# Attention, MoE and GLU on one core: token order scattered inside the GLU, GpSimd's weight splits whole and in other iterations

## The chip, the cores and the metric

The kernel runs on one core of a Trainium2 chip. The metric is the device time of one execution in microseconds (us). The engines are called as in the profile: PE is TensorE (matmuls; PEld its weight loads), DVE is VectorE, ACT is ScalarE, POOL is GpSimd and SP is SyncE, which here only issues DMAs. Each engine works through its own instructions in program order; semaphores tie them together.

## What is computed

Three stages follow each other, all in float32: sliding-window attention with four sink tokens, a top-1 mixture of eight experts with a capacity, and a gated linear unit (GLU).

```python
scores = where(is_sink | in_window, q @ k.T / sqrt(64), -1e9)    # 2 x 8 heads, 768 tokens
x = softmax(scores) @ v                                          # -> [1536, 512]

e = argmax(x @ w_gate, axis=1)                                   # top-1 of 8 experts
disp[e, counts[e]] = x[i]       # the first 384 tokens of each expert, in order of token
y = relu(disp @ w1) @ w2        # 512 -> 1024 -> 512
x[i] = gate_w[i] * y[e, pos[i]] # 0 for tokens over the capacity

out = (sigmoid(x @ w_gate2) * (x @ w_val)) @ w_out               # 512 -> 1536 -> 512
```

## The kernel before

Matmuls are float32 products made of three products each (`mm3`, lines 174 to 177): an operand is split into a high part and the rest. The split of a weight tile is `split_w` (lines 132 to 140): ACT copies the raw tile (`staged`, 128x1024) into the high half of a `pair` tile (L135), and another engine subtracts that from the raw tile into the low half (L140). Raw tiles come by DMA on SP's queue (`load_w`) into four stage buffers of two tiles each.

**Attention** (lines 180 to 684) goes through 12 tiles of 128 tokens, six for each of two sequences. A loop over `n` = 0 to 23 takes half the heads of tile `i = n // 2` in an iteration. In one iteration PE makes the `scores` of `n` (L288), the transposes of iteration n-1 (L321) and the products with `v` of n-2 (`pv`, L342, with a sink product L380); DVE adds the masks (L296) and ACT takes the exponentials (L307). An odd iteration ends with the sinks (`sink_gather`: two copies on ACT, L363, and a subtraction `psk` on DVE, L366, both of whose inputs lie in SBUF) and with `place` of tile i-2, whose first DVE instruction gives `pos_all` (L460) and frees the bank of PSUM that the next scores need. Iteration 15, the odd one of the second sequence's second tile, also splits that sequence's sink rows on DVE (`vsh`, L259 and L260).

POOL copies `v` at even iterations (`place_v`, L218), computes slot numbers, scales and scatters the rows of tile i-2 to the experts' slots in DRAM at odd ones (L467 to L481), and in ten iterations makes the split of one weight tile. These ten are picked by the list `splits` (line 578): from 6 on, without tile 6 (12 and 13) and without 15, so 6 to 11, 14, 16, 17 and 18. Two iterations after each, SP loads the tile that takes the place of the split one. When POOL makes a split, it is cut into four subtractions of 128x256.

**The token order.** A token's row in the experts' output differs from its row in the result. For each tile of tokens, `pi` (a sum of two tables, made by DVE) says where in the order its tokens went; POOL scatters the token numbers there, 128 at a time, by an indirect DMA into a table `idsd` in DRAM (`order_ids`, lines 705 to 712). In experts 1 to 6 one call makes two columns of `pi` and two scatters. After the last expert SP loads the whole table as `ids` (`load_ids`, L715), a DMA of 1,536 runs of 4 bytes.

**The experts** (lines 718 to 961) work through 128 to 384 rows each, with branches on the counts, while weights stream in.

**The GLU** (lines 980 to 1181) has three chunks of 512 rows and 12 steps in a chunk. A step `t` multiplies the chunk by a block of two weight matrices (`up`: 24 matmuls, then `g` on ACT and DVE, `gh` on ACT, `gl` on DVE), and then multiplies the step before by the output weights into four accumulators `acc0` to `acc3` (`down`: 12 matmuls). The accumulators are complete after the `down` of a chunk's last step, which runs in the first step of the next chunk; for the first chunk that is step 12, the thirteenth. There `finish` copies each accumulator into a buffer `o` (ACT for 0 and 2, DVE for 1 and 3; three buffers in all) and POOL scatters its rows to the result at the places in `ids` (L1065). The `down` of the next step, the 13th by number, starts the accumulators anew, `acc3` last.

Of the kernel before, what the change touches and what calls it, by code (L numbers as in the profile page):

```python
# [9 lines left out]
F32 = mybir.dt.float32  # L10
# [5 lines left out]
ALU = mybir.AluOpType  # L16
# [5 lines left out]
SUB = 1024  # L22
# [4 lines left out]
def kernel(  # L27
# [16 lines left out]
    nc = tc.nc  # L44
# [6 lines left out]
    NT = S // P  # L51
    NTILE = B * NT
# [8 lines left out]
    AHEAD = 10  # L61
# [31 lines left out]
    pi_a = const.tile([P, NTILE], F32, name="pi_a")  # L93
    pi_d = const.tile([P, NTILE], F32, name="pi_d")
    pi = const.tile([P, NTILE], I32, name="pi")
# [36 lines left out]
    def split_w(i, eng):  # L132

        raw, t = staged(i), pair[i // 2 % NDBL][:, :, i % 2 * SUB:(i % 2 + 1) * SUB]
        nc.scalar.copy(out=t[:, 0], in_=raw)  # L135

        n = 4 if eng is nc.gpsimd else 1
        for j in range(n):
            c = slice(j * SUB // n, (j + 1) * SUB // n)
            eng.tensor_sub(out=t[:, 1, c], in0=raw[:, c], in1=t[:, 0, c].bitcast(F32))  # L140

    def split_next(i, eng):

# [36 lines left out]
    def attention():  # L180
        with ExitStack() as st:
# [85 lines left out]
            NQ = 2 * NTILE  # L267
# [255 lines left out]
            for m, c in ((0, 0), (1, BW), (2, BW)):  # L523
# [3 lines left out]
                    out=blk, in_=blk, pattern=[[-1, P]], compare_op=ALU.is_ge, fill=MASKED,  # L527
# [46 lines left out]

            splits = [n for n in range(6, NQ) if n // 2 != NT and n != 2 * NT + 3][:AHEAD]
            for n in range(NQ):
                i, a = divmod(n, 2)  # L580
                if a == 0:
# [120 lines left out]
        )  # L702
        nc.vector.tensor_tensor(out=pi_a, in0=a, in1=pos_all, op=ALU.add)

    def order_ids(i0, i1):
        c = slice(i0, i1)
        nc.vector.tensor_tensor(out=pi[:, c], in0=pi_a[:, c], in1=pi_d[:, c], op=ALU.add)
        for i in range(i0, i1):
            nc.gpsimd.indirect_dma_start(
                out=idsd_v[i], out_offset=bass.IndirectOffsetOnAxis(ap=pi[:, i:i + 1], axis=0),  # L710
                in_=ids0[:, i:i + 1], in_offset=None, bounds_check=N - 1, oob_is_err=False,
            )

    def load_ids():
        nc.sync.dma_start(out=ids, in_=idsd.rearrange("(j p) o -> p (j o)", p=P))  # L715


    def experts(yh, yl):
        with ExitStack() as st:
# [188 lines left out]
            for e in range(E):  # L908
                w1a, w1b, w2a, w2b = (weights(4 * e + j) for j in range(4))
                m = 8 * e  # L910
                if e:
                    load_x_next(e + 2)
                    load_more(e)
                    split_next(m + 2, V)
                    split_next(m + 3, V)
                u = bank(ps_u, 0)
                go(products(u, x, w1a, True, True))
                ra = relu(u)
                if e:
                    put_y(e - 1, 0, yr)  # L920
                    split_next(m + 4, V)
                else:
                    cnt_x = counts([nc.sync.engine])
                    for j in range(1, E):
                        nc.sync.dma_start(
                            out=slots[j * ROWS:(j + 1) * ROWS, :][bass.ds(cnt_x[j], P), :], in_=zero)
                    load_more(e)
                    load_x_next(2)
                u = bank(ps_u, 0)
                b = products(u, x, w1b, True, True)  # L930
                go(b[:6])
                ha = turn_h(ra, 0)
                if e:
                    split_next(m + 5, V)
                go(b[6:])
                rb = relu(u)
                if e:
                    split_next(m + 6, V)
                if e + 1 < E:
                    x = turn_x(xs[e + 1], 0)  # L940
                y = bank(ps_y, 0)
                a = products(y, ha, w2a, True, False)
                go(a[:6])
                hb = turn_h(rb, 1)
                if e:
                    split_next(m + 7, V)
                go(a[6:])
                if e == 0:
                    cnt_e = counts([nc.tensor.engine, nc.scalar.engine, nc.vector.engine])
                    order(hp)  # L950
                elif e < 7:
                    order_ids(2 * (e - 1), 2 * e)
                fills = [partial(split_w, m + j, V) for j in (8, 9)] if 0 < e < E - 1 else []
                if e + 1 == E:
                    for q in range(4):
                        fills += [partial(whole, q, h * 512, h * 512 + 512) for h in range(2)]
                        if q < 2:
                            fills.append(partial(convert, q))
                yr = more_tiles(e, y, products(y, hb, w2b, False, True), fills)
                if 0 < e < E - 1:  # L960
                    load_w(m + 16)
                    load_w(m + 17)
            load_glu(4, 0)
            load_glu(5, 1)
            load_ids()
            fill_clock(5)
            for q in range(2, 4):
                convert(q)
# [11 lines left out]
    def glu(yh, yl):  # L980
        with ExitStack() as st:
# [36 lines left out]
            def up(n, r, w):  # L1018
                ch = n // NPAIR
                c = slice(r * P, (r + 1) * P)  # L1020
                cols = slice(ch * 512, ch * 512 + w)
                pss = []
                for j in range(2):
                    wh, wl = block(n, j)
                    ps = ps_g.tile([P, 512], F32, tag=f"g{j}", name=f"g{j}")[:, :w]
                    for k in range(KD):
                        mm3(ps, wh[:, k, c], wl[:, k, c], yh[:, k, cols], yl[:, k, cols], k == 0, k == KD - 1)
                    pss.append(ps)
                gh = gp.tile([P, 512], F32R, tag="gh", name="gh", bufs=3)
                gl = gp.tile([P, 512], F32R, tag="gl", name="gl", bufs=3)  # L1030
                g = gp.tile([P, 512], F32, tag="g", name="g")[:, :w]
                nc.scalar.activation(out=g, in_=pss[0], func=AF.Sigmoid)  # L1032
                nc.vector.tensor_tensor(out=g, in0=g, in1=pss[1], op=ALU.mult)  # L1033
                nc.scalar.copy(out=gh[:, :w], in_=g)  # L1034
                k = last_rows(w)
                nc.vector.tensor_sub(out=gl[:, :w - k], in0=g[:, :w - k], in1=gh[:, :w - k].bitcast(F32))  # L1036
                if k:
                    nc.vector.tensor_sub(
                        out=gh[:, w:w + k], in0=g[:, w - k:], in1=gh[:, w - k:w].bitcast(F32)
                    )  # L1040
                return gh, gl
# [48 lines left out]
            def run(t0, t1, w, half, before):  # L1090

                ch = t0 // NF
                held = []

                for m in range((w + P - 1) // P, 4):
                    put_out(ch * 4 + m, zero)
                for t in range(t0, t1):
                    pend = []
                    n, r = steps[t]
                    while half and len(pend) < 3:  # L1100
                        x, h = half[0]
                        if todo[x][0] > n + 2:
                            break
                        half.pop(0)
                        pend.append((x, h))
                    parts = [(x % 4, h * 512, h * 512 + 512) for x, h in pend]
                    for step in range(3):
                        conv_a(parts, step)
                    g = up(n, r, w)
                    for x, h in pend:  # L1110
                        conv_b(x % 4, todo[x][2], h * 512, h * 512 + 512, nc.vector)
                        if h and x + 4 < len(todo):
                            load_glu(todo[x + 4][1], x % 4)
                    if before and t < len(steps) - 2:
                        full = w if t > t0 else 512
                        for m in range((full + P - 1) // P):
                            down(t - 1, m, *before, full)
                        if t % NF == 0:
                            for m in range(4):
                                finish(t // NF - 1, m, full)  # L1120
                    held = (held + [g])[-3:]
                    before = g
                if t1 == len(steps):

                    ms = list(range((w + P - 1) // P))
                    if w % P:
                        ms = ms[-1:] + ms[:-1]
                    for m in ms:
                        down(t1 - 3, m, *held[0], w)
                    for m in ms:  # L1130
                        down(t1 - 2, m, *held[1], w)
                        down(t1 - 1, m, *held[2], w)
                        finish(ch, m, w, m == ms[-1])
                return before
# [117 lines left out]
```

## Time and profile before

| | |
|---|---|
| median of three runs | 642.01 us (640.71 to 644.28) |
| the profiled execution | 642.88 us |
| its span, first to last instruction | 641.0 us |
| mean granted TensorE clock | 0.977 of 2.4 GHz |
| attention / expert 0 / other experts / GLU, from about | 0 / 137 / 194 / 350 us |
| PE, DVE, ACT, POOL busy | 95%, 57%, 47%, 18% of the span |

The profile is of one execution. The page gives each engine's busy time, the clock that TensorE was granted and the DMA engines' load. The trace behind it gives each instruction's start and duration, in us from the span's start, and in brackets how long its engine had been idle before it and what ended that wait.

### The profile page before, as it was taken

To read this page: it belongs to the slowest core of one execution; us is meant where nothing else is said; L and a number is where in the kernel's file an instruction comes from. 1 tells how busy PE (TensorE), PEld (TensorE's weight loads), DVE (VectorE), ACT (ScalarE), POOL (GpSimd) and SP (SyncE) were. 2 spreads that over 40 slices of the span, in tenths; PEclk is the share of its full clock that TensorE was granted. 3 is DMA by queue.
4 is the path that set the end of the run, shared out by engine and by line. 5 is a ranking of instruction groups with operands and counts; after the bars stand their busy time and mean duration, and the time that the engine had idled before them with its cause. 6 is when DMAs were issued, how large, how long until landed. Compare 5 with 4: busy or idle time off the path is not lost.

```text
span 641.0 us, 9386 instructions
## 1 busy us (share of the span) xinstructions
PE 606.8 (95%) x3326; PEld 504.9 (79%) x3326; DVE 365.6 (57%) x884; ACT 303.0 (47%) x586; POOL 114.6 (18%) x191
## 2 busy tenths in 40 slices
PE   9999989999997889898799999999999999999995
PEld 4888888957876667686687788888888888999994
DVE  2565566544269446828567999993218921238811
ACT  3676666613268446737545655542214521225411
POOL 3169778360002010201000000000200000200002
PEclk9998989999999789989989999999999999999999
DMA  8999947033038965957944555453101530103001
GB/s 182 305 292 310 298 143 235 17 126 125 0 108 221 210 237 188 219 170 255 128 178 133 198 195 179 178 179 123 65 1 65 197 132 0 67 0 95 38 0 70
DMA packets 43630, 93.97 MB, mean 147 GB/s; under 512 B 5664, under 2 KB 24352, under 8 KB 39728
## 3 DMA queue, kind: packets, MB, share of 16 engines
q1 hardware_dynamic: 39872, 86.24, 45.8%
q0 software_dynamic: 2304, 6.09, 2.6%
q10 hardware_dynamic: 1392, 0.86, 0.6%
q8 instruction: 34, 0.56, 0.4%
q14 instruction: 28, 0.23, 0.1%
HBM read 82.63 MB, written 10.75 MB: 146 GB/s over the span
## 4 chain that ended last, share of the span: by engine, by line
PE 52%; issue 30%; DVE 6%; DMA 5%; ACT 5%; POOL 1%; SPq 0%; POOLq 0%; ACTq 0%; DVEq 0%
PE u L779 20%; PE pv L342 5%; PE g L176 4%; PE g L177 4%; PE g L175 4%; PE t L321 3%; PE s L288 2%; DMA xe<-slots 2%; PE idle L505 2%; DMA stage<-in_we_dram 2%; PE acc L177 2%; PE acc L176 2%; PE acc L175 2%; DVE pair L140 2%; ACT pt L307 1%
## 5 line engine op out<-in xcount | busy, mean ns | idle before, releaser
L176 PE MATMUL g<-yl,pair 128*128 128x512 f32 (+1 forms) x288 | 108.4, 376 | 0.3 <-DVE yl L812 0.3
L175 PE MATMUL g<-yh,pair 128*128 128x512 f32 (+1 forms) x288 | 108.4, 376 | 0.2 <-ACT yh L811 0.2
L177 PE MATMUL g<-yh,pair 128*128 128x512 f32 (+1 forms) x288 | 108.3, 376 | 0.0
L140 DVE TENSOR_TENSOR pair<-stage,pair 128x1024 fp32r<-128x1024 f32 x54 | 64.8, 1221 | 19.7 <-ACT pair L135 19.4
L779 PE MATMUL u<-pair,hh 128*128 128x512 f32 x224 | 66.1, 423 | 9.2 <-issue 8.0
L1034 ACT CAST gh<-g 128x512 fp32r<-128x512 f32 (+1 forms) x36 | 21.4, 594 | 110.1 <-DVE g L1033 106.1
L1033 DVE TENSOR_TENSOR g<-g,g 128x512 f32<-128x512 f32 (+1 forms) x36 | 23.5, 651 | 82.4 <-PE g L177 82.4
L135 ACT CAST pair<-stage 128x1024 fp32r<-128x1024 f32 x64 | 65.8, 1051 | 0.9 <-PE u L779 0.8
L779 PE MATMUL u<-pair,xh 128*128 128x512 f32 x224 | 62.9, 409 | 0.1
L175 PEld LDWEIGHTS g<-yh,pair 128*128 128x128 f32 x288 | 54.1, 188 | 9.4 <-ACT yh L811 0.7
L176 PEld LDWEIGHTS g<-yl,pair 128*128 128x128 f32 x288 | 54.1, 188 | 8.6 <-issue 0.6
L177 PEld LDWEIGHTS g<-yh,pair 128*128 128x128 f32 x288 | 54.1, 188 | 7.4
L307 ACT ACTIVATE pt<-sc,neg 128x260 f32<-128x260 f32 (+1 forms) x96 | 44.6, 491 | 30.8 <-DVE neg L296 30.2
L779 PEld LDWEIGHTS u<-pair,hh 128*128 128x128 f32 x224 | 43.2, 200 | 20.3 <-issue 10.8
L1065 POOL DMA_INDIRECT out_dram<-o,ids x11 | 10.8, 983 | 246.9 <-DVE gl L1036 151.6
L779 PEld LDWEIGHTS u<-pair,xh 128*128 128x128 f32 x224 | 43.1, 197 | 10.8 <-ACT xh L753 1.3
L177 PE MATMUL acc<-pair,gl 128*128 128x512 f32 x132 | 51.5, 390 | 0.0
L176 PE MATMUL acc<-pair,gh 128*128 128x512 f32 x132 | 51.4, 390 | 0.0
L175 PE MATMUL acc<-pair,gh 128*128 128x512 f32 x132 | 51.4, 389 | 0.0
L1032 ACT ACTIVATE g<-g 128x512 f32<-128x512 f32 (+1 forms) x36 | 20.5, 568 | 60.5 <-PE g L177 60.5
L342 PE MATMUL pv<-v,pts 128*128 128x73 f32 x352 | 43.2, 276 | 0.0
L342 PEld LDWEIGHTS pv<-v,pts 128*128 128x128 f32 x352 | 42.5, 197 | 0.1
(163 smaller groups left out, 1039.1 us busy)
## 6 DMA issues: line engine op xcount, KB each, us to landing
stage<-in_we_dram SPq DMA_DIRECT2D x64, 512.0 KB
stage<-in_wd_dram SPq DMA_DIRECT2D x30, 1024.0 KB
vraw<-in_vr_dram SPq DMA_DIRECT2D x11, 288.0 KB
kraw<-in_kd_dram SPq DMA_DIRECT2D x22, 132.0 KB
qraw<-in_qd_dram SPq DMA_DIRECT2D x22, 128.0 KB
vt<-in_vt_dram SPq DMA_DIRECT2D x11, 256.0 KB
slots<-zero SPq DMA_DIRECT2D x1, 2048.0 KB
xs<-slots SPq DMA_DIRECT2D x8, 256.0 KB
```

Source lines behind the costliest of these rows:

```text
L135: nc.scalar.copy(out=t[:, 0], in_=raw)
L140: eng.tensor_sub(out=t[:, 1, c], in0=raw[:, c], in1=t[:, 0, c].bitcast(F32))
L175: nc.tensor.matmul(ps, ah, bh, start=start, stop=False)
L176: nc.tensor.matmul(ps, ah, bl, start=False, stop=False)
L177: nc.tensor.matmul(ps, al, bh, start=False, stop=stop)
L307: nc.scalar.activation(out=pt_[i][:, h, :w], in_=scs_[n][j][:, :w], func=AF.Exp, scale=-1.0, bias=neg_[i][:, h:h + 1],)
L321: nc.tensor.transpose(tt[:, r, j], pt_[i][:, 4 * a + 2 * p + r, c:c + P], ident)
L342: nc.tensor.matmul(pv_[n][:, h], pts_[n, h // 2][:, h % 2, j], vb[kb][:, 4 * a + h], start=(h == 0 and j == 0), stop=(h == 3 and j == len( ...
L779: nc.tensor.matmul(ps, a, b, start=start, stop=stop)
L1032: nc.scalar.activation(out=g, in_=pss[0], func=AF.Sigmoid)
L1033: nc.vector.tensor_tensor(out=g, in0=g, in1=pss[1], op=ALU.mult)
L1034: nc.scalar.copy(out=gh[:, :w], in_=g)
```

## The change

Three things change. POOL's split is one subtraction of 128x1024. The list of iterations with a split leaves out 12 to 15 in place of 12, 13 and 15, so that it is 6 to 11 and 16 to 19. And `order_ids` makes all twelve columns of `pi` in one DVE instruction and issues all twelve scatters one after the other, in the GLU's step 10 behind `up`; `load_ids` stands in step 12.

```diff
@@ split_w
         nc.scalar.copy(out=t[:, 0], in_=raw)
-
-        n = 4 if eng is nc.gpsimd else 1
-        for j in range(n):
-            c = slice(j * SUB // n, (j + 1) * SUB // n)
-            eng.tensor_sub(out=t[:, 1, c], in0=raw[:, c], in1=t[:, 0, c].bitcast(F32))
+        eng.tensor_sub(out=t[:, 1], in0=raw, in1=t[:, 0].bitcast(F32))
@@ attention
-            splits = [n for n in range(6, NQ) if n // 2 != NT and n != 2 * NT + 3][:AHEAD]
+            splits = [n for n in range(6, NQ) if n // 2 not in (NT, NT + 1)][:AHEAD]
@@
-    def order_ids(i0, i1):
-        c = slice(i0, i1)
-        nc.vector.tensor_tensor(out=pi[:, c], in0=pi_a[:, c], in1=pi_d[:, c], op=ALU.add)
-        for i in range(i0, i1):
+    def order_ids():
+        nc.vector.tensor_tensor(out=pi, in0=pi_a, in1=pi_d, op=ALU.add)
+        for i in range(NTILE):
             nc.gpsimd.indirect_dma_start(
@@ experts
                     order(hp)
-                elif e < 7:
-                    order_ids(2 * (e - 1), 2 * e)
@@
             load_glu(5, 1)
-            load_ids()
             fill_clock(5)
@@ glu, run
                     g = up(n, r, w)
+
+                    if t == 10:
+                        order_ids()
+                    elif t == 12:
+                        load_ids()
                     for x, h in pend:
```

POOL's instructions in attention, from the copy of `v` in iteration 14 to the split of iteration 16, before; `pair` and `stage` are the split's tiles, `xg` the scaled rows, `slots` the experts' rows in DRAM:

```order
L218 COPY v<-vraw 128x8x64
L140 TENSOR_TENSOR pair_90<-stage_86,pair_90 128x256 x4
L455 TENSOR_TENSOR acc<-acc,oh_all 128x8
L467 TENSOR_SCALAR sl<-idf,pos_all 128x1
L471 TENSOR_SCALAR over<-pos_all 128x1
L475 TENSOR_SCALAR si<-over,sl 128x1
L443 TENSOR_SCALAR xg<-x,g 128x512
L481 DMA slots<-xg,si 4096x512
L217 MEMSET v 128x8
L218 COPY v<-vraw 128x8x64
L140 TENSOR_TENSOR pair_90<-stage_86,pair_90 128x256 x4
```

And now, the same stretch (the change's line numbers are 4 to 9 lower):

```order
L214 COPY v<-vraw 128x8x64
L451 TENSOR_TENSOR acc<-acc,oh_all 128x8
L463 TENSOR_SCALAR sl<-idf,pos_all 128x1
L467 TENSOR_SCALAR over<-pos_all 128x1
L471 TENSOR_SCALAR si<-over,sl 128x1
L439 TENSOR_SCALAR xg<-x,g 128x512
L477 DMA slots<-xg,si 4096x512
L213 MEMSET v 128x8
L214 COPY v<-vraw 128x8x64
L136 TENSOR_TENSOR pair_90<-stage_86,pair_90 128x1024
```

The split behind the first copy is gone, the tile that it made is made in iteration 16, and it is one instruction instead of four.

POOL's instructions from the last expert with an order to the first output scatters, before:

```order
L709 DMA idsd<-ids_67,pi 1536x1 x2
L742 UNCONDITIONAL_BRANCH
L879 UNCONDITIONAL_BRANCH
L1065 DMA out_dram<-o,ids 1536x512 x4
L1139 TENSOR_LOAD cnt_i
```

And now:

```order
L736 UNCONDITIONAL_BRANCH
L873 UNCONDITIONAL_BRANCH
L703 DMA idsd<-ids_67,pi 1536x1 x12
L1056 DMA out_dram<-o,ids 1536x512 x4
L1135 TENSOR_LOAD cnt_i
```

All twelve scatters of the order now stand right ahead of the first four output scatters. On DVE the sum that they need stands between `gl` of step 10 and `g` of step 11, two steps ahead of the copies of `acc1` and `acc3`:

```order
L1027 TENSOR_TENSOR gl<-g,gh 128x512
L701 TENSOR_TENSOR pi<-pi_a,pi_d 128x12
L1024 TENSOR_TENSOR g<-g,g_5951 128x512
L1027 TENSOR_TENSOR gl<-g,gh 128x512
L1024 TENSOR_TENSOR g<-g,g_5996 128x512
L1027 TENSOR_TENSOR gl<-g,gh 128x512
L1073 COPY o<-acc_5232 128x512
L1073 COPY o<-acc_5234 128x512
```

Before, there was no `pi` here; the row after `gl` was the next step's `g`.

## Rows read from the trace of the kernel before

**Rows 1.** Order of time, POOL, attention: start, duration (us), line, operation, idle before.
```profile
41.23 0.62 POOL L218 COPY v<-vraw 128x512 f32<-128x512 f32 x1 [4.01 <-DMA vraw<-in_vr_dram]
41.82 2.80 POOL L140 TENSOR_TENSOR pair<-stage,pair 128x256 fp32r<-128x256 f32 x4
...
51.99 2.79 POOL L140 TENSOR_TENSOR pair<-stage,pair 128x256 fp32r<-128x256 f32 x4
...
81.19 3.39 POOL L140 TENSOR_TENSOR pair<-stage,pair 128x256 fp32r<-128x256 f32 x4
```

**Rows 2.** Order of time, DVE, attention.
```profile
41.91 0.68 DVE L366 TENSOR_TENSOR psk<-pt,psk 128x32 fp32r<-128x32 f32 x1 [2.79 <-ACT psk L363]
...
52.42 1.78 DVE L366 TENSOR_TENSOR psk<-pt,psk 128x32 fp32r<-128x32 f32 x1 [2.85 <-ACT psk L363]
...
81.53 1.09 DVE L260 TENSOR_TENSOR vsh<-vsr,vsh 32x512 fp32r<-32x512 f32 x1
...
84.00 0.61 DVE L366 TENSOR_TENSOR psk<-pt,psk 128x32 fp32r<-128x32 f32 x1
```

**Rows 3.** Line L366 as a whole: shortest, median, longest in ns.
```profile
L366 DVE TENSOR_TENSOR psk<-pt,psk x10: 191/207/1785, 22.1 to 125.6; 128x32 fp32r<-128x32 f32 x10
```

**Rows 4.** Order of time, PE, attention: scores.
```profile
47.05 1.17 PE L288 MATMUL s<-kraw,qraw 64*128 64x132 f32 x16
...
54.34 1.00 PE L288 MATMUL s<-kraw,qraw 64*128 64x132 f32 x6 [1.26 <-DVE pos_all L460]
...
59.65 1.17 PE L288 MATMUL s<-kraw,qraw 64*128 64x132 f32 x16
...
81.82 0.72 PE L288 MATMUL s<-kraw,qraw 64*128 64x132 f32 x8
...
84.76 0.71 PE L288 MATMUL s<-kraw,qraw 64*128 64x132 f32 x6 [1.39 <-DVE pos_all L460]
...
90.05 1.17 PE L288 MATMUL s<-kraw,qraw 64*128 64x132 f32 x16
...
95.15 1.26 PE L288 MATMUL s<-kraw,qraw 64*128 64x132 f32 x16
```

**Rows 5.** Stretches: us, busy us (count) of PE, PEld, DVE, ACT, POOL; PEclk; DMA.
```profile
54.62:58.03 3.41, 3.41 (x20) 3.18 (x18) 2.66 (x15) 2.12 (x5) 2.94 (x7) 0.50 1.12 295
85.34:88.75 3.41, 3.41 (x18) 3.34 (x17) 2.35 (x15) 2.71 (x7) 3.00 (x5) 0.50 0.91 226
```

**Rows 6.** Groups by line and shape, POOL: busy us, mean ns, idle before.
```profile
L140 POOL TENSOR_TENSOR pair<-stage,pair 128x256 fp32r<-128x256 f32 x40 | 28.5, 743 | 1.1 <-DVE sum L387 1.0
...
L673 POOL TENSOR_TENSOR tmp<-kd,lower 128x64 f32<-128x64 f32 x1 | 0.3, 335 | 0.0
```

**Rows 7.** Order of time, GLU, around the end of the first chunk.
```profile
439.36 0.69 DVE L1036 TENSOR_TENSOR gl<-g,gh 128x512 fp32r<-128x512 f32 x1 [0.69 <-ACT gh L1034]
...
456.41 0.98 POOL L1065 DMA_INDIRECT out_dram<-o,ids  x1 [151.56 <-DVE gl L1036]
457.69 0.99 POOL L1065 DMA_INDIRECT out_dram<-o,ids  x1 [0.30 <-issue]
...
459.26 0.69 DVE L1082 COPY o<-acc 128x512 f32<-128x512 f32 x1 [2.29 <-DMA out_dram<-o,ids]
...
464.23 0.39 PE L175 MATMUL acc<-pair,gh 128*128 128x512 f32 x1
```

**Rows 8.** Order of time, experts: `pi`, its scatter, and the `ids` load.
```profile
193.08 0.15 DVE L707 TENSOR_TENSOR pi<-pi_a,pi_d 128x2 int32<-128x2 f32 x1
...
193.51 1.76 POOL L709 DMA_INDIRECT idsd<-ids,pi  x1 [49.70 <-DVE pi L707]
...
347.82 0.38 SPq L715 DMA_DIRECT2D ids<-idsd  x1
```

**Rows 9.** DMA, 347 to 353 us: GB/s in slices of 0.15 us.
```profile
GB/s 382 492 164 109 0 0 0 164 382 0 55 164 55 218 218 164 546 328 492 382 437 382 492 382 492 382 382 492 111 278 6 10 9 5 4 1 0 0 0 0
```

**Rows 10.** Stretches, as in rows 5, in the GLU's step 11.
```profile
440.00:448.00 8.00, 8.00 (x37) 6.63 (x36) 1.22 (x3) 1.22 (x2) 0.00 (x0) 1.00 0.02 8
```

## The prediction

> **What bounds the kernel now.** I read the page first, then the waits, then the order of time around them. TensorE (PE) is the engine that is busy nearly throughout, so time can only come from places where PE stands still or runs at half clock. The change touches three stretches: attention (to 137 us), the six experts that issue the token order, and the GLU around the end of its first chunk (456 us). In this last stretch PE never waits, and the DMA engines are all but idle [rows 10].
>
> In attention PE stands still twice for over a microsecond, each time in the scores that follow an odd iteration (9 and 15), both times released by VectorE's `pos_all` [rows 4]: 1.26 us before 54.34 and 1.39 us before 84.76. Right ahead of `pos_all` on VectorE stands `psk` (L366), a subtraction with two SBUF inputs. It takes 0.19 us at best, 0.21 in the median and 1.79 at worst [rows 3]. It is long only while GpSimd's split (L140, two SBUF inputs as well) is running: the split of iteration 8 runs from 51.99 to 54.78 [rows 1], and the `psk` of 52.42 ends at 54.20 [rows 2]; the split of iteration 14 runs from 81.19 to 84.58, and `vsh` (81.53) and `psk` (84.00) lie stretched inside it. So the two engines hold each other up. Behind both waits the granted clock is at the lower level (1.2 GHz) for 3.41 us [rows 5]. Scores start 5.10 us apart when nothing is wrong (90.05 to 95.15); 47.05 to 59.65 is two iterations and takes 12.60, 2.4 too much; 81.82 to 90.05 is one and takes 8.23, 3.1 too much [rows 4].
>
> **Part 1: no split in iterations 14 and 15.** Before, 14 had one and 15 none; now both are free and iteration 19 gets the tenth. Without it `psk` waits only for its copies on ScalarE and, with 0.2 us of its own and without the stretched `vsh` ahead, ends near 83.3 instead of 84.6: scores resume 1.3 us earlier. PE's idle there falls from 1.39 to about 0.1, so I expect no clock drop. Half of 3.41 is 1.7 us of work lost to it; some of that time PE would wait for ScalarE's `pskT` instead, and I take 0.8. Sum -2.1 us. Bounds: -1.3 (VectorE's part alone) and -3.1 (the whole excess). The tenth split costs ScalarE one cast and GpSimd one split in iteration 19, behind which GpSimd has none left: 0. The weight loads behind the last four splits leave SP's queue one or two iterations later; expert 1, the first to need them, is some 70 us further on: 0.
>
> **Part 2: whole splits.** No row shows a 128x1024 subtraction on GpSimd. A 128x256 takes 0.743 us, a 128x64 product 0.335 [rows 6]: 2.1 ns an element, so 0.335 + 960 x 2.1 ns = 2.4 us. Bounds: 2.79 (four pieces as they run now [rows 1], no saving), and 2.15 (with 0.697 us, a quarter of 2.79, for the piece). I take 2.4, by the durations. The 0.4 us saved per split are worth nothing alone; what counts is where `psk` meets a split.
>
> In iteration 7 the split of 6 starts at 41.82, right behind a copy that had waited for its load, and `psk` at 41.91 [rows 1, 2]; `psk` got in after one piece and ended at 42.59. Behind a whole split it ends near 44.2, 1.6 us later, PE stands still about as long, the clock drops, and with 0.8 for that: +2.4. In iteration 9 `psk` therefore comes 2.4 us later, at 54.8. GpSimd, on which the splits of 6 and 7 each became 0.4 us shorter, starts the split of 8 at 51.99 - 0.8 = 51.2 and ends it at 53.6: the two no longer meet, and the excess of 2.4 goes. Net 0.0. In 11 and 19 GpSimd has the same or a larger lead: 0.
>
> What the pieces are worth: the `psk` of 52.42 passed the ends of two pieces (52.7 and 53.4) and got in only behind the third. The Trainium skill (SBUF — State Buffer, Who interferes with whom) says that a VectorE instruction with two SBUF inputs contends with a GpSimd instruction that reads SBUF, and that the one that issues second blocks until the first has finished. By that rule pieces would have let it in at 52.7, and a whole split can only lengthen a meeting; the trace agrees for 41.91 (0.7 us) and not for 52.42. What the rule makes of this change is rival B.
>
> **Part 3: the order out of the experts.** Six `pi` of 0.15 us leave VectorE and twelve scatters leave GpSimd [rows 8], which has nothing else there. `pi` stands ahead of a weight split; on the path or not, it is worth 0 to 6 x 0.15 = -0.9; taken -0.2. The `ids` load no longer runs among the GLU's first weight loads, for which PE never waits: 0.
>
> **Part 4: the order into the GLU.** The new `pi` follows the `gl` of the eleventh step, which ends at 440.05 [rows 7]; VectorE has nothing behind it until the next step, so `pi` itself is free. GpSimd starts 0.3 us after `pi` (193.08 + 0.15 to 193.51 [rows 8]): 440.5. Twelve scatters at the step of 456.41 to 457.69 [rows 7], 1.28 us: the twelfth starts at 440.5 + 11 x 1.28 = 454.6 (455.3 if the first takes 1.76 as in [rows 8]). From a scatter's start to what waited for it went 2.85 us (456.41 to 459.26), so SP may issue the `ids` load at 457.4 to 458.2. That load, 1,536 pieces of 4 bytes, went out at 347.82 among weight loads [rows 8] and its last pieces passed near 352.3 [rows 9]: 4.5 us. On idle DMA engines the nearest row is the scatter's 2.85; I take 3.2. So `ids` is there at 460.7, and the first output scatter starts then instead of at 456.41. The fourth `o` copy (there are three buffers) waits 2.85 us for it and ends at 460.7 + 2.85 + 0.69 = 464.25 instead of 459.95. It frees `acc3`, which PE needs at 464.23 [rows 7]: the slack of 4.3 us is used up to the hair, +0.3 with a semaphore. Bounds: 0, and 458.2 + 4.5 + 2.85 + 0.69 = 466.25, a wait of 2.0 us that also drops the clock (1.7): +3.7. Queued behind that copy on VectorE is the next step's `g`, whose product PE needs one step (8 us) later: covered. Nothing waits behind SP's and GpSimd's new waits, since the next load and scatter come steps later.
>
> **Sum.** -2.1 + 0.0 - 0.2 + 0.3 = -2.0 us. The profiled execution took 642.88 us (span 641.0 and 1.9 around it), 0.9 above the median of 642.01 and well inside the runs' 640.71 to 644.28. So 640.9 for an execution like it, and 640.0 at the level of the median, which I give.
>
> **Rivals.** A, the meetings vanish altogether. `psk` and the split of 6 start 0.09 us apart, and they hang on different things (a load here, ScalarE there). If `psk` is first, 7 costs nothing; with splits near 2.79 us the split of 8 would start behind `psk` in 9 too, and the excess of 2.4 goes: 640.0 - 2.4 = 637.6. For it: the narrow margin. Against: both must fall right.
>
> B, slower: `psk` meets a whole split in 7 and in 9. Decided by the start of the split of 8: if the copy ahead of it has to wait for its load past about 54 (the one of 41.23 waited 4.01 us [rows 1]), 9 waits up to 2.4 us instead of 1.6. Then +2.4 and +0.8 stand against -2.1, -0.2 and +0.3: 642.0 + 1.2 = 643.2. Against it: GpSimd's lead grows by 0.8 us while `psk` comes later.
>
> C, slower: the chain of `ids` is late. From a wait of 1.3 us on, after which the clock fell in both cases above, it costs 1.3 + 1.7 = 3.0 to 3.7 in place of 0.3: 642.7 to 643.4. Against it: the DMA engines are idle there.
>
> D, the gain of part 1 does not reach the end, because something behind attention (scatters, first loads of the experts) is late anyway: 642.0.
>
> **How the numbers follow.** Forecast 0.45, A 0.20, B 0.13, C 0.12, D 0.10. The forecast's own bounds, -3.1 to -1.3 in part 1 and 0 to -0.9 in part 3, with some 1.5 us between runs, give 638 to 642. The range reaches through most of A below and through B and C above: 636.8 to 644.0. What a measurement of this kernel can tell from no change is about 0.5%, 3.2 us. Faster than 638.8: most of A and the forecast's lower end, 0.30. Slower than 645.2: B and C together, or one beyond its bounds, 0.10. The same: 0.60.
>
> **What would show it.** In the profile after: no stretched VectorE instruction around 81 to 85 and no half-clock stretch near 85; one near 44 in place of the one near 55 (A: neither, B: both); single splits of 2.2 to 2.8 us; twelve scatters in a row in the GLU, and a PE wait under 0.5 us at the `acc3` of the next step (C: over 1.3 us, with half clock behind it); PE's waits in the experts as before. A wait above 2 us there, or no gain between 77 and 93 us, would make the prediction wrong.

## The result, and the profile after

The changed kernel takes 625.55 us in the median of four runs (624.61 to 627.28), beside 642.08 for the kernel before: a ratio of 0.9743, 95% interval 0.9706 to 0.9779. It is 16.5 us faster; the forecast was 2 us, and the time lies below the range. The profiled execution has a span of 623.2 us (before: 641.0) and a mean granted clock of 0.986 (before: 0.977).

Where the 17.8 us between the two spans came from is read off two marks on PE: the first and the last group of transposes that turn an expert's result `y`. Order of time, PE, before and then after:

```profile
166.17 0.60 PE L809 MATMUL t<-ident,yr 128*128 128x128 f32 x4
...
350.77 0.66 PE L809 MATMUL t<-ident,yr 128*128 128x128 f32 x4 [0.29 <-ACT yr L800]
```

```profile
163.31 0.60 PE L803 MATMUL t<-ident,yr 128*128 128x128 f32 x4
...
324.45 0.65 PE L803 MATMUL t<-ident,yr 128*128 128x128 f32 x4 [0.29 <-ACT yr L794]
```

Up to the first mark 2.9 us are gained. Between the marks, in the experts, it is 184.6 before and 161.1 after: 23.5 us gained. From the last mark to the end, the GLU, it is 290.2 before and 298.7 after: 8.5 us lost. The forecast had 2.1, 0.2 and -0.3 for the three.

**The experts.** Before, PE stood still five times for more than 1.5 us between 200 and 325 us, 16.8 us in all, each stand with 3.4 or 6.8 us of the lower clock level behind it. Two of them, in order of time:

```profile
211.15 2.04 PE L779 MATMUL u<-pair,hh 128*128 128x512 f32 x4 [6.06 <-issue]
...
228.58 0.98 PE L750 MATMUL t<-ident,xe 128*128 128x128 f32 x4 [2.45 <-DVE pi L707]
```

After, four of the five are gone; of the one that ended at 302.96 (1.93 us) 1.29 are left, with no lower clock behind them. The reader should now look at the DMA engines over the same stretch of time: the busy tenths and GB/s from 193 to 223 us, in 40 slices of 0.75 us, before and then after.

```profile
DMA  9899998999661522155999999999999394999432
GB/s 284 333 415 377 382 388 317 344 172 137 46 66 55 82 82 55 74 79 186 426 404 388 399 410 404 432 399 252 230 164 71 49 71 71 82 104 76 16 22 38
```

```profile
DMA  9977999999998999988769999999999999994000
GB/s 317 328 262 300 366 347 421 385 404 388 350 289 262 366 410 361 224 311 246 295 268 311 344 361 336 396 404 421 404 421 300 371 382 399 317 333 186 38 0 0
```

Before, what the engines move falls from some 380 GB/s to under 90 from 200.5 to 206.5 us, some 5 us behind the first two scatters (193.51 in [rows 8] and 195.6), and again from 215.5 us on, behind the next two (206.9 and 208.9). In five of the second hollow's ten slices the engines are marked busy nine tenths, and move 71 to 104. In the stretch from 187 to 222 us (columns as in [rows 5]) that makes 222 GB/s at a busy share of 0.96 before and 322 at 0.89 after:

```profile
187.00:222.00 35.00, 28.62 (x132) 22.80 (x131) 24.29 (x27) 23.51 (x32) 5.43 (x4) 0.90 0.96 222
```

```profile
187.00:222.00 35.00, 34.34 (x170) 27.53 (x169) 28.72 (x30) 26.89 (x37) 0.00 (x0) 1.00 0.89 322
```

**The GLU.** Order of time after, the new chain, to be held against [rows 7]:

```profile
414.09 1.02 POOL L703 DMA_INDIRECT idsd<-ids,pi  x1 [273.14 <-DVE pi L701]
...
428.26 0.98 POOL L703 DMA_INDIRECT idsd<-ids,pi  x1 [0.30 <-issue]
...
435.95 0.38 SPq L709 DMA_DIRECT2D ids<-idsd  x1
...
439.92 0.98 POOL L1056 DMA_INDIRECT out_dram<-o,ids  x1 [10.68 <-issue]
...
442.78 0.69 DVE L1073 COPY o<-acc 128x512 f32<-128x512 f32 x1 [8.87 <-DMA out_dram<-o,ids]
...
443.52 0.80 PE L171 MATMUL acc<-pair,gh 128*128 128x512 f32 x1 [5.45 <-DVE o L1073]
```

PE stands for 5.45 us. From 441.4 on the clock is at the lower level (1.2 GHz) for 6.8 us; the first 2.1 of them still belong to the stand, and in the rest PE works for 4.68 us at half its pace, which costs another 2.3. Together that is 7.8 of the 8.5 us that the marks show; of what is left 0.6 lies behind PE's last matmul, which starts 6.95 us ahead of the end before and 7.51 after:

```profile
441.40:448.20 6.80, 4.68 (x11) 3.75 (x12) 1.98 (x3) 0.62 (x1) 2.75 (x3) 0.50 0.40 154
```

**Attention.** Against [rows 1 to 4]: the split is one instruction of 2.37 us, no `psk` meets one, and the scores of 81.82 and 90.05 now start at 81.72 and 87.54. `psk` as a whole, then in order of time:

```profile
L362 DVE TENSOR_TENSOR psk<-pt,psk x10: 191/193/193, 25.1 to 122.7; 128x32 fp32r<-128x32 f32 x10
```

```profile
40.64 2.37 POOL L136 TENSOR_TENSOR pair<-stage,pair 128x1024 fp32r<-128x1024 f32 x1 [0.43 <-ACT pair L135]
...
44.93 0.19 DVE L362 TENSOR_TENSOR psk<-pt,psk 128x32 fp32r<-128x32 f32 x1 [2.79 <-ACT psk L359]
...
54.93 0.19 DVE L362 TENSOR_TENSOR psk<-pt,psk 128x32 fp32r<-128x32 f32 x1 [2.84 <-ACT psk L359]
...
81.72 0.72 PE L284 MATMUL s<-kraw,qraw 64*128 64x132 f32 x8
...
87.54 1.17 PE L284 MATMUL s<-kraw,qraw 64*128 64x132 f32 x16
```

### The profile page after: what moved, and what is told of

Read it like the earlier page. It is cut to its first block, busy times and chain, and to the rows that moved or that the text cites. A ratio compares the mean times of both kernels' runs of the same rounds, so it can differ in the third digit from the quotient of the medians.

```text
span 623.2 us, 9350 instructions
## 1 busy us (share of the span) xinstructions
PE 599.0 (96%) x3326; PEld 499.4 (80%) x3326; DVE 361.0 (58%) x879; ACT 302.4 (49%) x586; POOL 107.1 (17%) x161
## 5 line engine op out<-in xcount | busy, mean ns | idle before, releaser
L773 PE MATMUL u<-pair,hh 128*128 128x512 f32 x224 | 61.7, 401 | 2.8 <-ACT pair L135 1.5
L773 PE MATMUL u<-pair,xh 128*128 128x512 f32 x224 | 60.5, 397 | 0.1
L703 POOL DMA_INDIRECT idsd<-ids,pi x12 | 11.8, 983 | 276.5 <-DVE pi L701 273.1
L303 ACT ACTIVATE pt<-sc,neg 128x260 f32<-128x260 f32 (+1 forms) x96 | 44.6, 491 | 26.4 <-DVE neg L292 26.3
L773 PEld LDWEIGHTS u<-pair,hh 128*128 128x128 f32 x224 | 40.5, 188 | 13.2 <-issue 4.4
L773 PEld LDWEIGHTS u<-pair,xh 128*128 128x128 f32 x224 | 40.8, 188 | 10.2 <-ACT xh L747 1.7
```

Of the source, the lines that this page charges most:

```text
L303: nc.scalar.activation(out=pt_[i][:, h, :w], in_=scs_[n][j][:, :w], func=AF.Exp, scale=-1.0, bias=neg_[i][:, h:h + 1],)
L703: nc.gpsimd.indirect_dma_start(out=idsd_v[i], out_offset=bass.IndirectOffsetOnAxis(ap=pi[:, i:i + 1], axis=0), in_=ids0[:, i:i + 1], in_of ...
L773: nc.tensor.matmul(ps, a, b, start=start, stop=stop)
```

## The experiments

The theory to test, S: the twelve scatters, issued while the experts' weights stream in, hold up the weights' transfers, and PE stands still for weights and rows that come late. Rivals: T, the stands went because the splits moved the experts' start; V, VectorE's six additions of `pi` did it. All runs in one table; "experts" and "GLU" are the stretches between the marks above in the profiled execution, ratios are to the kernel before, measured beside each on the same chip.

| kernel | median us | ratio (95%) | experts us | GLU us |
|---|---|---|---|---|
| before | 642.08 | 1 | 184.6 | 290.2 |
| changed | 625.55 | 0.974 (0.971-0.978) | 161.1 | 298.7 |
| order_only | 628.02 | 0.978 (0.969-0.986) | 161.0 | 299.3 |
| splits_only | 640.36 | 0.997 (0.993-1.002) | 185.2 | 290.2 |
| pi_in_experts | 639.05 | 0.996 (0.991-1.000) | 182.1 | 290.2 |
| adds_only | 624.89 | 0.975 (0.971-0.978) | 163.1 | 299.0 |
| scat_e2 | 629.75 | 0.979 (0.973-0.985) | 170.6 | 295.0 |
| direct12 | 641.30 | 1.002 (0.999-1.006) | 177.4 | 299.4 |
| rows64 | 627.16 | 0.976 (0.970-0.982) | 164.3 | 299.7 |
| rows512 | 627.71 | 0.979 (0.972-0.985) | 161.1 | 300.2 |
| act12 | 649.98 | 1.013 (1.007-1.019) | 184.3 | 299.1 |
| order_t6 | 618.06 | 0.963 (0.954-0.971) | 162.8 | 293.5 |
| order_t8 | 623.61 | 0.970 (0.964-0.977) | 162.1 | 296.1 |
| order_t9 | 621.35 | 0.971 (0.965-0.976) | 161.0 | 294.3 |
| wide_experts | 618.29 | 0.964 (0.961-0.968) | 161.1 | 290.3 |
| wide_glu | 617.31 | 0.962 (0.958-0.966) | 161.3 | 290.3 |
| wide_before | 617.58 | 0.962 (0.954-0.969) | 161.3 | 290.2 |

**One part alone.** order_only puts the old splits and list back into the changed kernel, splits_only puts the new ones into the kernel of before.

> Only the order is moved, as in the changed kernel; the splits and their list are those of before. The experts of the changed kernel are 23.5 us shorter than those of before (from the first to the last transposed put: 184.6 us before, 161.1 after), its GLU 8.6 us longer, its attention 2.9 us shorter. Theory S (the twelve scatters in the experts hold up the weights' transfers, and TensorE stands still for them): the experts lose 23.5 and the GLU gains 8.6 without the splits, 642.1 - 23.5 + 8.6 = 627.2, range 625.5 to 630, and the stands of TensorE over 1.5 us between 200 and 325 us are gone. Theory T (the stands go because the splits let the experts start at another time against the weights' stream): the stands stay, and the GLU's 8.6 are added: 650.7.

> Only the splits and their list are changed, as in the changed kernel; the order stays in the experts and the ids load at the GLU's start. Theory S: only the attention's 2.9 us go, 639.2, range 637 to 641, and the stands of TensorE in the experts stay. Theory T: the attention's 2.9 and the experts' 23.5 go, 615.7.

S holds and T falls: the experts are 161.0 with the old splits and 185.2 with the new ones. The splits' own share, 0.997, can't be told from nothing.

**The additions, or the scatters.** pi_in_experts has six `order_pi(2 * (e - 1), 2 * e)` in the experts and the scatters' code in the GLU.

> The changed kernel, with the addition of the positions put back into the second to seventh expert in its six parts; the twelve scatters stay in the GLU. Theory S: 625.6, as the changed kernel, within 1.5 us. Theory V (the six additions on VectorE, which come between the splits of the weights, and not the scatters, are what held the experts up): up to 23.5 us slower than the changed kernel, 640 to 649.

It was slower, as V has it, but it isn't a test of V: the scatters ran in the experts again, where GpSimd's queue holds nothing ahead of them. The trace of pi_in_experts, first and last start:

```profile
L706 POOL DMA_INDIRECT idsd<-ids,pi x12: 977/980/1756, 189.0 to 296.2; - x12
```

adds_only cuts the tie: the additions write a tile `pix` of their own.

```diff
+    def extra(i0, i1):
+        c = slice(i0, i1)
+        nc.vector.tensor_tensor(out=pix[:, c], in0=pi_a[:, c], in1=pi_d[:, c], op=ALU.add)
...
+                elif e < 7:
+                    extra(2 * (e - 1), 2 * e)
```

> The changed kernel, with six additions of two columns each, of the same operands as those of before, put back into the second to seventh expert; they write a tile that nothing reads, and no scatter follows them. Needed because in pi_in_experts GpSimd, which has nothing else queued, issued the scatters right behind the additions, at 189.0 to 296.2 us, so that both went back together. Theory S (the scatters): 625.6, as the changed kernel, within 1.5 us, and no stand of TensorE over 1.5 us in the experts. Theory V (the additions on VectorE): 639, as pi_in_experts.

As S has it: 624.89. The one stand over 1.5 us in its experts is of 1.65 us at 281.4, where the changed kernel has one of 1.29; with 3.4 us of lower clock behind it, it makes the 2.0 us by which these experts are longer. Kernels without any addition there stand longer at this place too (1.56 us in order_t6, 2.39 in order_t8), so at most 2.0 of the 23.5 us are left to V. So the "DVE pi" that the profile of before names as the releaser of a stand of 2.45 us was the last to come, but not what cost the time.

**A dose of two.** scat_e2 has `order_ids(2, 4)` back at e == 2, and (0, 2) and (4, 12) in the GLU.

> The changed kernel, with two of the twelve scatters (those of the third and fourth tile of tokens) and their addition back in the third expert, the other ten in the GLU. If each scatter costs the same, 23.5 / 12 = 2.0 us, the experts (from the first to the last transposed put) go from 161.1 to 165.0 us, with one stand of TensorE of 2 to 3 us and a half-clock stretch some 18 us behind the scatters; the GLU's chain is two scatters shorter, 2.6 us of its 5.45 us stand: 625.6 + 3.9 - 2.6 = 626.9. If the cost comes only when one pair of scatters meets the next one's backlog (pairs lie 13 to 30 us apart in the kernel of before), nothing is lost in the experts: 623.0.

Neither number: the experts are 9.5 us longer than the changed kernel's, not 3.9 and not 0. Behind the two scatters (at 202.92 and 204.98) PE stood for 4.72 us at 214.5 and then worked 5.67 us at the lower clock, which costs another 2.8. Held against the changed kernel, PE's instructions start 7.4 us later behind this stand. The other 2.1 us come at a second stand, of 1.84 us before 289.88 and with 3.4 us of lower clock behind it. That is the place where the changed kernel stands for 1.29 and adds_only, with no transfer in its experts, loses 2.0; so the pair of scatters is charged with 7.4 us, and the 2.1 stay open. Order of time, and the lower clock behind the first stand:

```profile
219.23 1.09 PE L745 MATMUL t<-ident,xe 128*128 128x128 f32 x4 [4.72 <-issue]
...
289.88 1.01 PE L774 MATMUL u<-pair,hh 128*128 128x512 f32 x2 [1.84 <-issue]
```

```profile
218.10:224.90 6.80, 5.67 (x16) 4.64 (x17) 1.92 (x2) 1.53 (x2) 0.00 (x0) 0.50 1.04 420
```

DMA of scat_e2, 193 to 223 us in slices of 0.75 us, with the hollow from 210 to 217:

```profile
DMA  8989999997968999977899999996464149999999
GB/s 333 339 336 374 320 352 442 366 366 295 251 273 289 317 350 300 350 257 252 284 287 240 216 123 82 60 30 30 36 38 27 16 142 426 399 404 421 431 437 415
```

So the cost is not a fixed 2.0 us per scatter: one pair made one hollow in the stream and one stand, and cost 7.4 us; six pairs cost 23.5.

**What of a scatter it is.** direct12 is adds_only with plain transfers of a column behind each addition; rows64 and rows512 write rows of 16 and 128 numbers in place of one; act12 issues direct12's transfers from ScalarE.

```diff
+        for i in range(i0, i1):
+            nc.gpsimd.dma_start(out=idsd_v[NTILE + i][N + i * P:N + (i + 1) * P, :], in_=pix[:, i:i + 1])
```

> The changed kernel, with the same six additions in the experts, each followed by two plain transfers from GpSimd's queue that write the 128 numbers of a column to 512 consecutive bytes of DRAM that nothing reads, instead of a scatter. If what costs is the small writes of 4 bytes, however addressed: as pi_in_experts, 639 (636 to 642). If it is the scattering (each of the 128 writes at an address of its own, read from a tile): 625.6, as the changed kernel.

> As direct12 (641.3, its experts 177.4 us against 161.1 of the changed kernel), but each of the twelve plain transfers writes 128 rows of 64 bytes instead of 128 single numbers of 4 bytes; as many packets, from the same queue at the same places. Theory P (what costs is the packets of GpSimd's queue beside a full stream, whatever their size): experts 177, time 641. Theory Q (what costs is that a write is as small as 4 bytes): experts 161 to 163, time 626 to 628; the bytes themselves, 12 x 8 KB, are 0.3 us of a stream of 350 GB/s.

> As rows64, with rows of 512 bytes: 12 x 64 KB, 0.79 MB, is 2.2 us of a stream of 350 GB/s. Theory P: experts 177 or more, time 641 to 644. Theory Q: experts 161 to 165, time 626 to 630. If rows64 costs and this doesn't, the bound lies between 64 and 512 bytes.

> As direct12, 4 bytes a packet, but issued on ScalarE's queue instead of GpSimd's. Theory Q (the small writes): experts 177, time 641. If it is GpSimd's queue that is served at the cost of the weights' queue: experts 161 to 165 (ScalarE gives some 0.3 us for each of twelve issues, which lies beside its slack), time 626 to 629.

The stretch 187 to 222 us of direct12, rows64 and act12:

```profile
187.00:222.00 35.00, 30.59 (x139) 24.48 (x139) 25.14 (x29) 23.97 (x32) 2.35 (x5) 0.90 1.03 264
```

```profile
187.00:222.00 35.00, 34.36 (x170) 27.30 (x168) 31.23 (x36) 28.49 (x38) 3.33 (x6) 1.00 0.94 332
```

```profile
187.00:222.00 35.00, 28.41 (x137) 22.09 (x135) 26.46 (x30) 24.86 (x33) 0.00 (x0) 1.00 0.84 218
```

DMA of act12, 187 to 222 us in slices of 0.875 us:

```profile
GB/s 262 225 183 332 309 375 403 146 52 0 0 14 75 28 19 23 94 328 414 403 405 403 421 412 417 384 403 258 84 108 103 61 159 225 94 47 225 215 330 276
```

The scattering isn't needed (direct12 costs 16.3 us in the experts without it), nor is GpSimd's queue (act12 costs 23.2, with hollows as before). act12 missed its number, 177 us of experts and 641 in all: ScalarE, which copies the weights as well, also waits for each addition and issues the transfers, and the trace records a column as 128 packets there and as 16 on GpSimd's queue; which of these makes the 6.9 us beyond direct12 was not separated. As many writes of 64 or of 512 bytes move 16 and 128 times the bytes and cost 3.2 and 0.0 us, where the additions without any transfer (adds_only) show 2.0; the 3.2 come at the same late stand, 2.59 us in rows64. What costs is the writes of 4 bytes.

The trace's records of single packets show how. Between the marks SP's queue moves some 7,650 packets of 2 KB or more, which take 0.16 us in the median. In the kernel before 118 of them took over 2 us (the longest 7.2), in scat_e2 20, in direct12 116 and in act12 67; none did in the changed kernel, adds_only, rows64, rows512 and the three kernels with wide rows below. The scatters' own packets took some 0.015 us. So the stream was not short of work: its own packets were held up.

The Trainium skill (DMA: Bandwidth & Descriptors, Why small descriptors are slow) names two fixed overheads: some cycles for each packet, and 32 bytes of descriptor for each DMA operation. Neither falls when a row is widened from 4 bytes to 64, so by it rows64 would lose what direct12 loses; the runs say otherwise (164.3 against 177.4). No size between 4 and 64 bytes was run, nor writes of 4 bytes that lie 64 apart, so the width of the writes and their distance are not told apart; and no run shows what such a write does in the memory.

**The same cause in the GLU.** order_t6, order_t8 and order_t9 change `t == 10` and `t == 12` to 6 and 9, 8 and 10, 9 and 11.

> The changed kernel, with the order in the GLU's seventh step (t == 6) and the ids load in its tenth (t == 9). The GLU's stand of 5.45 us with its 6.8 us of half clock (8.6 us together) should go, since the ids would land some 35 us earlier: 625.6 - 8.6 = 617.0. There the GLU's own weights still come, at a mean of 190 GB/s, about half of what the stream moves when it is full. Theory S with a stream that has room: 617, range 616 to 619. Theory S where a scatter costs the same beside any stream (23.5 us by twelve scatters is 2.0 us each): up to 617 + 23.5 = 640. If the 5.45 us are not the ids' chain but something else at the finish of a chunk: 625.

> The changed kernel, with the order in the GLU's tenth step (t == 9) and the ids load in its twelfth (t == 11), one step of some 8 us earlier. The GLU's last weights are issued at 409.6 us in the changed kernel, so the scatters (from some 405 us) meet only the last one or two transfers of the stream. The ids then land 8 us earlier, against a stand of 5.45 us: the stand and its half clock go, 625.6 - 8.6 = 617.0 (616 to 618), less than order_t6's 618.1 if the 2.74 us for which TensorE stood there (weights that came late beside the scatters) are gone. If the last weights come late here too: 619 to 621.

> The changed kernel, with the order in the GLU's ninth step (t == 8) and the ids load in its eleventh (t == 10). In order_t9 the scatters began at 410.0 us, only 4.1 us ahead of the changed kernel's, and TensorE still stood for 2.23 us; another step of 4 to 5 us takes that away too. They begin at some 405 us, beside the last two transfers of the GLU's weights, which end at 412. If these come in time nevertheless: 625.6 - 8.6 = 617.0 (616 to 618). If they starve as in order_t6 (1 MB took 13 us beside the scatters there, TensorE stood 2.74 us): 618 to 620.

order_t6 came in at 618.06, as S with room has it, though the scatters (385.1 to 408.8 us) starve the stream here as well; the GLU merely has weights in hand for most of it. PE stood once, for 2.74 us before 404.45, and the GLU is 3.3 us longer than before's. DMA of order_t6, 380 to 412 us in slices of 0.8 us:

```profile
DMA  9999500049995339958015999877879973524999
GB/s 410 440 420 420 215 0 20 0 72 154 338 72 20 20 20 41 41 41 41 10 31 215 401 350 61 72 72 154 133 103 82 92 62 62 62 20 164 441 318 164
```

order_t9 and order_t8 missed 617: they start the scatters 4.1 and 10.0 us earlier than the changed kernel, beside the last weights, and the `ids` load could go only 2.7 and 2.0 us earlier (433.29 and 433.98). In order_t8 the tenth scatter itself waited 7.49 us for one ahead of it to land. Of PE's 5.45 us, 2.23 and 3.61 were left.

**Wider rows for the order itself.** The edit that all of this points to, in the changed kernel with the order at its old places (wide_experts), in the changed kernel (wide_glu) and in the kernel of before (wide_before):

```diff
-    idsd = dram.tile([N, 1], I32, name="idsd")
+    idsd = dram.tile([N, 16], I32, name="idsd")
-    ids0 = const.tile([P, NTILE], I32, name="ids0")
+    ids0 = const.tile([P, NTILE + 15], I32, name="ids0")
...
-                in_=ids0[:, i:i + 1], in_offset=None, bounds_check=N - 1, oob_is_err=False,
+                in_=ids0[:, i:i + 16], in_offset=None, bounds_check=N - 1, oob_is_err=False,
...
-        nc.sync.dma_start(out=ids, in_=idsd.rearrange("(j p) o -> p (j o)", p=P))
+        nc.sync.dma_start(out=ids, in_=idsd[:, 0:1].rearrange("(j p) o -> p (j o)", p=P))
```

> The order back at its places in the experts and the ids load back at the GLU's start, as before; but each scatter writes rows of 64 bytes (the id and fifteen numbers that nothing reads) instead of 4, and the ids load reads the first number of each row. Splits and list as in the changed kernel. Theory Q (4-byte writes starve the stream, wherever they are addressed): the experts keep the changed kernel's 161.1 us (161 to 163), the GLU gets back before's 290.2: 625.6 - 8.6 = 617.0, range 616 to 619. Rival R (scattered addresses, or the index reads of a scatter, cost on their own beside a full stream; direct12 lost 16.3 us in the experts, pi_in_experts 21.0, so 4.7 could be theirs): 617 + 4.7 = 621.7. Rival: the scatter's packets cost as they did with 4 bytes: 640.

> The changed kernel with 64-byte rows in its scatters, which stay in the GLU's eleventh step. In the changed kernel the last scatter was issued at 428.3 us and the ids load could go at 435.9: the landing took 7.6 us in a stretch in which the engines moved next to nothing. If small writes are slow to land by themselves, 64-byte rows land in the 2.86 us in which the output's scatters landed: the ids come 4.7 us earlier, and of the stand of 5.45 us some 0.7 and of the half clock half or all is left: 618 to 621. If the landing is the scatter's own and not the size's: 625.6.

> The kernel of before with nothing changed but the width of the order's rows: 64 bytes a scatter write instead of 4, and the ids load reads the first number of each row. Splits, list and every place are those of before. If the 4-byte writes are the whole cause of the experts' stands, the experts go from 184.6 us to 161.1 (160 to 163) with attention and GLU as before: 642.0 - 23.5 = 618.5, range 617 to 621. If the splits had a share in the experts' gain after all: 621 to 630.

All three come to 617 to 618 us, ahead of both kernels, with 161 us of experts and 290 of GLU. Scatters of 64 bytes at their old places cost nothing that shows here, so rival R falls. In wide_glu the last scatter, of 429.69, has landed by 431.89, 2.2 us later, where the changed kernel took 7.7 (428.26 to 435.95); the expectation of 2.86 was even too long, and the whole stand is gone:

```profile
429.69 0.98 POOL L704 DMA_INDIRECT idsd<-ids,pi  x1 [0.30 <-issue]
...
431.89 0.38 SPq L710 DMA_DIRECT2D ids<-idsd  x1
```

Beside the stream, too, the landing is shorter. From issue to landing (shortest, median, longest) in the kernel before, then in wide_experts:

```profile
DMA to landing us min/median/max: 9.5/11.5/16.1
```

```profile
DMA to landing us min/median/max: 5.7/6.1/6.7
```

wide_before shows that the order need not move at all: one row's width is worth 0.962, more than the whole change.

## Why the prediction was wrong

**Part 3 failed, and with it the size of the whole.** It counted what the order takes on its engines, 0.15 us of VectorE six times and a GpSimd "which has nothing else there", and bounded it at -0.9. It is 23.5 us, all of it in the DMA engines, of which part 3 said nothing. The instruction count was right; what a scatter puts on the queues was not priced. The prediction said rightly that time can only come from where PE stands still or runs at half clock, and counted the experts among the stretches that the change touches; but none of its terms has the 16.8 us of stands and the five low-clock stretches there, as it took the experts' waits to stay as before. Four of the five stands lay behind scatters, with a hollow in the GB/s between.

**Part 4 had the right chain and one wrong term.** GpSimd's start (414.09, where 440.5 less the 26.3 us that the GLU now starts earlier is 414.2), the step of 1.28 and the output scatter's 2.86 came out as put. The scatter's landing was taken from the output's scatter of 2 KB rows, 2.85, and was 7.7; the `ids` load was taken at 3.2 and was 3.97. These add 4.85 + 0.77 = 5.6 to a chain that, as put, used its slack up to the hair, and PE stood for 5.45. With 2.3 for the clock it is 7.8 (8.5 by the marks) in place of 0.3, beyond the bound of 3.7: the bound rested on the same 2.85. Rival C was the right mechanism at under half of its size. wide_glu, where the rows are 64 bytes, is the term's test: landing 2.2, no stand.

**Part 1 was right as far as one execution tells; part 2 came out as rival A has it, by luck.** The whole split is 2.37 us (taken 2.4). From the scores of 81.7 to those of the next iteration it is 5.82 us where it was 8.23, 2.4 less (taken 2.1), and no half clock lies behind. No `psk` met a split, so the two iterations from 47.05 [rows 4], now from 49.57, take 10.01 us in place of 12.60, and nothing came in 7, where `psk` came at 44.93, 3 us later than before and long after the split of 6. But all of attention was 3.0 us late by then (scores of 24.26, before 21.25): PE had waited 1.53 us for `kraw` at 12.46, where it waited 0.41 before, with 6.8 us of lower clock behind. That wait came and went between kernels that are alike there, so the change did not make it; it is also why gains of 2.6 and 2.4 and some small steps leave only 2.9 at the first mark.

In two kernels without that delay whole splits did meet `psk`. In wide_experts it met the split of 6 and ended with it, 1.42 us long, near the forecast (1.6); but PE stood only 0.83 us and no lower clock lay behind, where part 2 put 2.4.

```profile
40.54 2.35 POOL L136 TENSOR_TENSOR pair<-stage,pair 128x1024 fp32r<-128x1024 f32 x1
```

```profile
41.52 1.42 DVE L362 TENSOR_TENSOR psk<-pt,psk 128x32 fp32r<-128x32 f32 x1 [2.79 <-ACT psk L359]
```

In wide_glu `psk` met the split of 8, as rival B has it for iteration 9, and PE stood for 2.31 us with 3.4 us of lower clock behind:

```profile
52.35 2.83 DVE L362 TENSOR_TENSOR psk<-pt,psk 128x32 fp32r<-128x32 f32 x1 [2.00 <-ACT psk L359]
```

```profile
55.33 1.23 PE L284 MATMUL s<-kraw,qraw 64*128 64x132 f32 x6 [2.31 <-DVE pos_all L456]
```

How much of parts 1 and 2 reaches the end (rival D) stays open: splits_only is 0.997 with an interval over 1, and wide_experts and wide_before, which differ by the splits and their list, are equal within their intervals.

**Sum.** Forecast -2.1 + 0.0 - 0.2 + 0.3; by the marks -2.9 - 23.5 + 8.5 = -17.9, the 17.8 of the spans.

## What to carry to other kernels

Price a moved DMA by what it does to the queues beside it, not by the engine that issues it; where PE stands still, read the GB/s row ahead of the stand, since busy engines that move little point at the packets of someone else. Before looking for a better place for 4-byte writes beside a stream, widen them (here to 64 bytes, with fifteen numbers that nobody reads). And a landing time is to be taken from a transfer whose rows are as wide.

## What the runs showed of the hardware

- Two scatters, 256 writes of 4 bytes, beside a stream of some 300 GB/s pushed it to 16 to 82 GB/s for some 6 us, about 6 us after they were issued, and cost 7.4 us of the experts' time (scat_e2). With rows of 64 bytes in as many writes the stream moved 332 GB/s over the stretch from 187 to 222 us, where it moved 222 before (rows64).
- It comes from either queue (GpSimd 177.4 us of experts, ScalarE 184.3, without: 161.1), and without scattered addresses.
- The 4-byte writes land slowly even where the engines are idle: 7.7 us from the start of the last of twelve scatters, 2.2 us with 64 bytes.
- The engines' busy share does not show it: 0.96 with 222 GB/s, 0.89 with 322. What the 4-byte writes hold up is the packets of the stream, 118 of which took over 2 us between the marks before and none after; their own took some 0.015. What in the engines or the memory makes such a write so dear was not settled.
